# The zero column's term as a three-row matmul in the first sixteen steps, with ScalarE copying the product out of PSUM

## The chip, the cores and the metric

One core of a Trainium2 chip runs the kernel. The metric is device time in microseconds; for the kernel before it is 1673.05 us, the median of three runs. The engines are TensorE (PE in the profile, with PEld for its weight loads), VectorE (DVE), ScalarE (ACT), GpSimd (POOL) and SyncE (SP, which only issues DMAs here). Each works through its own instructions strictly in program order; semaphores hold an instruction back until what it needs is there.

## The reference, cut to what matters

```python
def _attn_ref(x):                       # x: 8 x 3072 x 256
    X = np.fft.fft(x, axis=1)
    X = np.fft.fft(X, axis=2)
    return X.real.astype(np.float32)

def _moe_ref(x, w_in, w_out):           # w_in 256 x 2048, w_out 2048 x 256
    h = x @ w_in
    sp = np.where(h > 20.0, h, np.log1p(np.exp(np.minimum(h, 20.0))))
    g = h * np.tanh(sp)                 # Mish
    return (g @ w_out).astype(np.float32)
```

The second function is applied to every row of the first one's result, 24576 rows in all.

## The kernel before, in words

The FFT along the columns (256 long) is folded into the weights: `make_wc` multiplies `w_in` with cosine and sine tables and gives `wch`, `wsh` (rounded to the matmul format) with the rests `wcl`, `wsl`. The FFT along the sequence is done by folds (sums and differences on VectorE and GpSimd) and matmuls with a table `dft`. Each of the 8 batches gives 3 chunks of 1024 tokens in mirrored pairs, held as two arrays P and Q: for one token of a pair the hidden value is P+Q, for the other P-Q.

A step takes one of the 16 blocks of 128 hidden units of a chunk; there are 384 steps, and the first chunk has steps 0 to 15. In step s `mm1` makes P in PSUM tile `pa` and Q in `pb` (three matmuls each: high times high, low times high, high times low part). `make_h` has three VectorE instructions: L848 adds to P the term of the column with index 0, which the folded weights do not hold (a token vector `p0b` times one number per hidden unit, `wc0`), and writes to SBUF; L849 adds Q, L850 subtracts it. ScalarE then applies Mish to the 1024 values (L958). Four steps later `split` rounds the result to `gh` on ScalarE (L858) and takes the rest `gl` on VectorE (L859; for steps 12 and later on GpSimd), and six steps later `mm2` (L869) multiplies with the second weights.

The order on each engine is written by hand: the main loop, and a table `EARLY` that says after which step the preparation of the weights and the folds of the first batch are placed. Entries with step -1 stand ahead of the loop. The 64-bit weights come as integer pairs; `conv` makes floats of them in three parts: part 0 on VectorE (L589, L590), part 1 on ScalarE (L592, L593), part 2 on VectorE and GpSimd (L595 to L597). `make_wl` (L626, L627) and `split_out` (L632, L633) make rests. All of this lies in the first 150 us, between the steps of the first chunk. `other_chunks` prepares the second chunk in steps 12 to 15 (its ScalarE instruction is L482).

At the start `zero`, a tile of zeros, is filled by GpSimd (L775); `warm` multiplies it with itself on TensorE (three matmuls, six rows of the profile) before and after `make_mids` (L646 to L659). `eye`, an identity matrix, comes by DMA as the third of ScalarE's queue. The first instruction of GpSimd that is no fill is L361 in `pairs0`. In the order of instructions a row ISA stands directly ahead of it; in the profile its two parts are called MODIFY_POOL_CONFIG.

Of the kernel before, what the change touches and what calls it, by code (L numbers as in the profile page):

```python
# [10 lines left out]
F32 = mybir.dt.float32  # L11
F32R = mybir.dt.float32r
# [3 lines left out]
ALU = mybir.AluOpType  # L16
# [72 lines left out]
def _tables():  # L89
# [46 lines left out]

SPLIT_V = 12
RH = 6

FOLD_AT = (19, 10, 44)  # L140
FIRST_AT = (44, 45)
# [133 lines left out]
def fft_moe(ctx, tc, x, col_d, mids_d, w_in, w_out, cs_d, dft_d, ysel_d, eye_d, out, single_d):  # L275
    nc = tc.nc
    V, A, G, T, SP = nc.vector, nc.scalar, nc.gpsimd, nc.tensor, nc.sync
    ctx.enter_context(tc.manual_schedule())

    def pool(name, bufs=1, **kw):  # L280
        return ctx.enter_context(tc.tile_pool(name=name, bufs=bufs, **kw))

    cp = pool("const")
# [23 lines left out]
    wsh = cp.tile([128, FF], F32R, name="wsh")  # L307
    wsl = cp.tile([128, FF], F32R, name="wsl")
    woh = cp.tile([128, NF, D], F32R, name="woh")
    wol = cp.tile([128, NF, D], F32R, name="wol")  # L310
    wc0 = cp.tile([128, NF], F32, name="wc0")
    ends = cp.tile([128, NB], F32, name="ends")
    ends0 = cp.tile([128, NB], F32, name="ends0")
    last2 = cp.tile([128, 2], F32R, name="last2")
    pe = cp.tile([NB, 1], F32, name="pe")

    place = [0, 0]

    def small(p, n, k=1):
        place[k] += n  # L320
        return hring[:p, RH - k, place[k] - n:place[k]]

# [7 lines left out]
    eye = small(128, 128)  # L330
# [142 lines left out]
    def mixed(v):  # L473

        return v.rearrange("p a s -> p s a")

    def placed(v):

        return v.rearrange("p (s a) -> p a s", a=2)
# [78 lines left out]
    p0b = {}  # L558
# [8 lines left out]
    raws, conv_w = {}, {}  # L567

    def room(kind, i):

        if kind == "in" and i in (2, 3):
            tu = gp.tile([128, 1024], F32, tag="gl", name="wtu")
            return gp.tile([128, 1024], F32, tag="gh", name="wraw"), tu[:, :512], tu[:, 512:]
        ring, j = PLACES[kind, i]
        r = (wring if ring == "w" else xring)[:, int(j)]
        return r[:, :1024], r[:, 1024:], otp.tile([128, 512], F32, tag="ot", name="wu")

    def load_w(kind, i):
        r, t, u = raws[kind, i] = room(kind, i)
# [2 lines left out]
    def conv(kind, i, part, eng="G"):  # L582

        r, t, u = raws[kind, i]
        lo, hi = (r.bitcast(I32).rearrange("p (n t) -> p n t", t=2)[:, :, j] for j in range(2))
        ti, ui = t.bitcast(I32), u.bitcast(I32)
        if part == 0:

            V.tensor_scalar(ui, hi, 20, 0x7FF, op0=ALU.logical_shift_right, op1=ALU.bitwise_and)  # L589
            V.tensor_single_scalar(ti, hi, 0xFFFFF, op=ALU.bitwise_and)  # L590
        elif part == 1:
            A.activation(ui, ui, AF.Relu, scale=2.0 ** 23, bias=-896.0 * 2 ** 23)  # L592
            A.activation(t, ti, AF.Copy, scale=2.0 ** -20, bias=1.0)  # L593
        else:
            V.scalar_tensor_tensor(ui, hi, -2 ** 31, ui, op0=ALU.bitwise_and, op1=ALU.bitwise_or)  # L595
            V.scalar_tensor_tensor(t, lo.bitcast(U32), 2.0 ** -52, t, op0=ALU.mult, op1=ALU.add)
            ENG[eng].tensor_tensor(t, t, u, op=ALU.mult)  # L597
            conv_w[kind, i] = t

    win_w = {}  # L600

    def make_wc(q):

# [20 lines left out]
    def make_wl(q):  # L624
        sl = slice(512 * q, 512 * q + 512)
        V.tensor_tensor(wcl[:, sl], win_w.pop(("lo", q, 0)), wch[:, sl], op=ALU.subtract)  # L626
        V.tensor_tensor(wsl[:, sl], win_w.pop(("lo", q, 1)), wsh[:, sl], op=ALU.subtract)  # L627

    def split_out(g):
        w = conv_w.pop(("out", g)).rearrange("p (f j) -> p f j", f=2)  # L630
# [5 lines left out]
    sp = {}  # L636
# [78 lines left out]
    def first_p0():  # L715

        pa = psacc.tile([128, 512], F32, tag="acc3", name="p0")
        def all_rows(v):
            return v[:, 0:1].to_broadcast([v.shape[0], 128])

        even = const(0, 0, 0)
        T.matmul(pa[:, 0:128], all_rows(xt[:, 0, 1, 0]), even[:, 0:128], start=True, stop=True)
        T.matmul(pa[:, 128:256], all_rows(xt[:, 0, 0, 0]), even[:, 128:256], start=True, stop=False)
        T.matmul(pa[:, 128:256], all_rows(xm[:, 0, 0]), alt[0:1, 128:256], start=False, stop=True)
        for c in range(2):
            T.matmul(pa[:, 256:512], all_rows(xt[:, 1, c, 0]), const(c, 1, 0), start=c == 0, stop=c == 1)
        p0b[0] = p2.tile([128, 512], F32, tag="p0b", name="p0b")
        A.copy(placed(p0b[0]), pa.rearrange("p (a s) -> p a s", a=2))


    G.memset(alt, 0.0)
# [14 lines left out]
    load_x(0, 3)  # L746
    load_w("in", 2)
    load_w("in", 3)


    uv = fp.tile([128, 2, 2, 2, 128], F32, tag="e", name="uv")
    eo = fp.tile([128, 2, 2, 128], F32, tag="o", name="eo")
# [64 lines left out]
    def chunk0(par, part):  # L817
# [1 line left out]

    parts = dict(chunk0=chunk0, put_mids=lambda: put_mids(0))  # L820
    parts.update({g.__name__: g for g in (
        make_mids, warm, first_p0, add_n1, fold_z, pairs0, sums0, load_w, conv, make_wc, make_w0, make_wl, split_out, col_fold, col_z, col_cs)})
    early = {}
    for t, g, args in EARLY:
        early.setdefault(t, []).append(lambda g=parts[g], args=args: g(*args))
# [6 lines left out]
    def mm1(s):  # L832
        ch, f = divmod(s, NF)
        q = chunks[ch]
        fs = slice(128 * f, 128 * f + 128)
        pa, pb = ps("pa"), ps("pb")
        for dst, wh, wl, n in ((pa, wch, wcl, "p"), (pb, wsh, wsl, "q")):
            dst = dst.rearrange("p (s a) -> p s a", a=2)
            T.matmul(dst, wh[:, fs], mixed(q[n + "h"]), start=True, stop=False)  # L839
            T.matmul(dst, wh[:, fs], mixed(q[n + "l"]), start=False, stop=False)  # L840
            T.matmul(dst, wl[:, fs], mixed(q[n + "h"]), start=False, stop=True)  # L841
        return pa, pb

    def make_h(s, pab):
        pa, pb = pab
        ch, f = divmod(s, NF)
        h = hring[:, s % RH]
        V.scalar_tensor_tensor(h[:, 0:512], p0b[ch], wc0[:, f:f + 1], pa, op0=ALU.mult, op1=ALU.add)  # L848
        V.tensor_tensor(h[:, 512:1024], h[:, 0:512], pb, op=ALU.add)  # L849
        V.tensor_tensor(h[:, 0:512], h[:, 0:512], pb, op=ALU.subtract)  # L850

    def split(s):

        h = hring[:, s % RH]
        gh = gp.tile([128, 1024], F32R, tag="gh", name="gh")
# [83 lines left out]
    for tau in range(NS + LAG_M):  # L939
        b, r = divmod(tau, 3 * NF)  # L940
# [8 lines left out]
        if tau < NS:  # L949
            make_h(tau, pab)  # L950
# [6 lines left out]
        if tau < NS:  # L957
            A.activation(hring[:, tau % RH], hring[:, tau % RH], AF.Mish)  # L958
            for f in early.pop(tau, []):
                f()  # L960
            other_at = OTHER_AT if b else OTHER0_AT
            if r in other_at:
                i = other_at.index(r)
# [7 lines left out]
            if fold_q:  # L971
                goal += pace
                while fold_q and spent + fold_q[0][0] / 2 <= goal + 1e-9 or fold_q and r == FOLD_AT[2]:
                    cost, f = fold_q.pop(0)
# [41 lines left out]
```

## Time and profile before

| | |
|---|---|
| median of three runs | 1673.05 us (1672.95 to 1673.29) |
| the profiled execution, its own time | 1674.39 us |
| its span in the profile | 1672.6 us |
| TensorE's matmuls busy | 1630.5 us, 97% of the span |
| VectorE / ScalarE / GpSimd busy | 1122.9 / 862.7 / 1153.5 us |

The profiled execution's time is 1.8 us above its span and 1.34 us above the median. Shares over the whole span say little about the first 150 us, where the change lies.

### The profile page before, as it was taken

To read this page: it belongs to the slowest core of one execution; us is meant where nothing else is said; L and a number is where in the kernel's file an instruction comes from. 1 tells how busy PE (TensorE), PEld (TensorE's weight loads), DVE (VectorE), ACT (ScalarE), POOL (GpSimd) and SP (SyncE) were. 2 spreads that over 40 slices of the span, in tenths; PEclk is the share of its full clock that TensorE was granted. 3 is DMA by queue.
4 is the path that set the end of the run, shared out by engine and by line. 5 is a ranking of instruction groups with operands and counts; after the bars stand their busy time and mean duration, and the time that the engine had idled before them with its cause. 6 is when DMAs were issued, how large, how long until landed. Compare 5 with 4: busy or idle time off the path is not lost.

```text
span 1672.6 us, 20901 instructions
## 1 busy us (share of the span) xinstructions
PE 1630.5 (97%) x7534; PEld 1403.6 (84%) x7534; DVE 1122.9 (67%) x1680; ACT 862.7 (52%) x968; POOL 1153.5 (69%) x654
## 2 busy tenths in 40 slices
PE   7778999999999999999999999999999999999999
PEld 4456888888888888888888888888888888888887
DVE  7998776666766767567766667667666667655453
ACT  3445555555555555555555555545554555554454
POOL 1444987588856877578866877578766788655566
PEclk8889999999999999999999999999999999999999
DMA  4212000300002000300002000020002000000000
GB/s 185 77 51 83 32 26 7 107 33 1 28 10 103 32 1 32 107 1 32 26 7 108 32 1 32 27 82 32 14 19 108 1 32 26 7 32 8 25 26 25
DMA packets 25376, 67.58 MB, mean 40 GB/s; under 512 B 3141, under 2 KB 3618, under 8 KB 25274
## 3 DMA queue, kind: packets, MB, share of 16 engines
q1 hardware_dynamic: 24474, 64.91, 10.7%
q8 instruction: 60, 0.98, 0.2%
q10 hardware_dynamic: 800, 1.35, 0.2%
q14 instruction: 42, 0.34, 0.1%
HBM read 40.97 MB, written 25.27 MB: 40 GB/s over the span
## 4 chain that ended last, share of the span: by engine, by line
PE 92%; DVE 6%; POOL 1%; issue 0%; DMA 0%; ACT 0%; DVEq 0%; ACTq 0%; POOLq 0%
PE acc L869 58%; PE pa L839 5%; PE pb L840 5%; PE pa L840 5%; PE pb L839 5%; PE pb L841 5%; PE pa L841 5%; PE pa L454 1%; PE pb L454 1%; DVE gl L859 1%; DVE hring L848 1%; DVE hring L849 1%; DVE wu L595 0%; DVE wu L589 0%; DMA hring<-table_ysel_dram 0%
## 5 line engine op out<-in xcount | busy, mean ns | idle before, releaser
L859 POOL TENSOR_TENSOR gl<-hring,gh 128x1024 fp32r<-128x1024 f32 x372 | 888.1, 2387 | 412.4 <-ACT gh L858 410.5
L858 ACT CAST gh<-hring 128x1024 fp32r<-128x1024 f32 x384 | 402.1, 1047 | 665.4 <-PE acc L869 647.6
L869 PE MATMUL acc<-gh,wol 128*128 128x512 f32 x1536 | 583.8, 380 | 2.9 <-POOL wol L633 2.9
L869 PE MATMUL acc<-gh,woh 128*128 128x512 f32 x1536 | 583.9, 380 | 0.6 <-ACT woh L632 0.6
L848 DVE SCALAR_TENSOR_TENSOR hring<-p0b,wc,pa 128x512 f32<-128x512 f32 x384 | 286.4, 746 | 371.7 <-PE pa L841 355.8
L958 ACT ACTIVATE hring<-hring 128x1024 f32<-128x1024 f32 x384 | 404.3, 1053 | 34.3 <-DVE hring L850 25.2
L869 PE MATMUL acc<-gl,woh 128*128 128x512 f32 x1536 | 406.2, 379 | 0.0
L869 PEld LDWEIGHTS acc<-gh,wol 128*128 128x128 f32 x1536 | 291.3, 190 | 45.1 <-POOL wol L633 3.6
L869 PEld LDWEIGHTS acc<-gh,woh 128*128 128x128 f32 x1536 | 291.4, 190 | 42.6 <-ACT woh L632 1.0
L869 PEld LDWEIGHTS acc<-gl,woh 128*128 128x128 f32 x1536 | 290.6, 189 | 41.9 <-POOL gl L859 0.5
L849 DVE TENSOR_TENSOR hring<-hring,pb 128x512 f32<-128x512 f32 x384 | 264.1, 688 | 42.7 <-DVE hring L848 1.8
L850 DVE TENSOR_TENSOR hring<-hring,pb 128x512 f32<-128x512 f32 x384 | 263.7, 687 | 13.3
L839 PE MATMUL pa<-h,wch 128*128 128x512 f32 x384 | 155.4, 405 | 7.2 <-DVE hring L848 5.0
L839 PE MATMUL pb<-h,wsh 128*128 128x512 f32 x384 | 147.2, 383 | 5.2 <-ACT h L482 3.5
L840 PE MATMUL pb<-l,wsh 128*128 128x512 f32 x384 | 146.7, 382 | 0.3 <-POOL l L483 0.3
L840 PE MATMUL pa<-l,wch 128*128 128x512 f32 x384 | 146.8, 382 | 0.0
L841 PE MATMUL pb<-h,wsl 128*128 128x512 f32 x384 | 146.6, 382 | 0.0
L841 PE MATMUL pa<-h,wcl 128*128 128x512 f32 x384 | 146.6, 382 | 0.0
L839 PEld LDWEIGHTS pa<-h,wch 128*128 128x128 f32 x384 | 73.3, 191 | 20.1 <-DVE hring L848 5.6
L839 PEld LDWEIGHTS pb<-h,wsh 128*128 128x128 f32 x384 | 73.1, 190 | 18.3 <-ACT h L482 3.9
L840 PEld LDWEIGHTS pb<-l,wsh 128*128 128x128 f32 x384 | 73.2, 191 | 11.1 <-POOL l L483 0.6
L841 PEld LDWEIGHTS pa<-h,wcl 128*128 128x128 f32 x384 | 73.4, 191 | 10.6
(255 smaller groups left out, 1154.2 us busy)
## 6 DMA issues: line engine op xcount, KB each, us to landing
xring<-x_dram SPq DMA_DIRECT2D x32, 768.0 KB
out_dram<-ot SPq DMA_DIRECT2D x96, 256.0 KB
p0b<-p_d SPq DMA_DIRECT2D x23, 256.0 KB
wring<-w_out_dram SPq DMA_DIRECT2D x5, 512.0 KB
wring<-w_in_dram SPq DMA_DIRECT2D x3, 512.0 KB
xring<-w_in_dram SPq DMA_DIRECT2D x3, 512.0 KB
xring<-w_out_dram SPq DMA_DIRECT2D x3, 512.0 KB
wraw<-w_in_dram SPq DMA_DIRECT2D x2, 512.0 KB
```

The costliest lines, as they stand in the source:

```text
L454: T.matmul(dst, lhs(c), const(c, par, sine), start=c == 0, stop=c == 1)
L839: T.matmul(dst, wh[:, fs], mixed(q[n + "h"]), start=True, stop=False)
L840: T.matmul(dst, wh[:, fs], mixed(q[n + "l"]), start=False, stop=False)
L841: T.matmul(dst, wl[:, fs], mixed(q[n + "h"]), start=False, stop=True)
L848: V.scalar_tensor_tensor(h[:, 0:512], p0b[ch], wc0[:, f:f + 1], pa, op0=ALU.mult, op1=ALU.add)
L849: V.tensor_tensor(h[:, 512:1024], h[:, 0:512], pb, op=ALU.add)
L850: V.tensor_tensor(h[:, 0:512], h[:, 0:512], pb, op=ALU.subtract)
L858: A.copy(gh, h)
L859: (V if s < SPLIT_V else G).tensor_tensor(gl, h, gh, op=ALU.subtract)
L869: T.matmul(acc[i].rearrange("p (s a) -> p s a", a=2), w[:, f, 128 * d:128 * d + 128], mixed(g.rearrange("p (a s) -> p a s", a=2)[:, :, 256 ...
L958: A.activation(hring[:, tau % RH], hring[:, tau % RH], AF.Mish)
```

## The change: what it does

In steps 0 to 15 the zero column's term is no longer added by VectorE. A fourth matmul with three rows (the weight's high part, its low part, its high part again, against the token vector's high, high and low part) adds it to `pa`, and ScalarE copies the finished `pa` to SBUF. VectorE makes only the sum and the difference. `make_rows` gathers the three weight rows for four steps at a time, with two matmuls against a selector `pick` and a copy; `p0_row` makes the token rows. `pick` and a factor `less` are made on GpSimd from `eye`. From step 16 on all is as before. The scratch of `conv` is now taken when part 0 runs, not when the load is issued.

```diff
+    pa = pa.rearrange("p (a s) -> p a s", a=2)
+    ph = p2.tile([128, 512], F32R, tag="p0b", name="ph")
+    A.copy(placed(ph[:3]), pa[:3])
+    sp["row"] = ph[:3], pa[:3]
+
+def p0_row():
+    ph, pa = sp["row"]
+    V.scalar_tensor_tensor(placed(prow), placed(ph), less, pa, op0=ALU.mult, op1=ALU.add)
...
+def make_rows(q):
+    sl = slice(512 * q, 512 * q + 512)
+    pw = psacc.tile([128, 512], F32, tag="acc3", name="pr") if q == 0 else ps("pb")
+    for k, w in enumerate((wsh, wsl)):
+        T.matmul(pw[:3], pick[:, 3 * k:3 * k + 3], w[:, sl], start=k == 0, stop=k == 1)
+    wrow[q] = otp.tile([128, 512], F32R, tag="ot", name="wrow")[:3]
+    A.copy(wrow[q], pw[:3])
...
     load_w("in", 2)
     load_w("in", 3)
+    G.tensor_single_scalar(less, eye[:3, 2:3], -1.0, op=ALU.mult)
+    for i in range(6):
+        G.tensor_single_scalar(pick[:, i:i + 1], eye[:, 127:128], float(i in (0, 2, 4)), op=ALU.mult)
...
-            T.matmul(dst, wl[:, fs], mixed(q[n + "h"]), start=False, stop=True)
+            row = s < ROWS and n == "p"
+            T.matmul(dst, wl[:, fs], mixed(q[n + "h"]), start=False, stop=not row)
+            if row:
+                T.matmul(pa, wrow[f // 4][:, 128 * (f % 4):128 * (f % 4) + 128], prow, start=False, stop=True)
...
-        V.scalar_tensor_tensor(h[:, 0:512], p0b[ch], wc0[:, f:f + 1], pa, op0=ALU.mult, op1=ALU.add)
+        if s < ROWS:
+            A.copy(h[:, 0:512], pa)
+        else:
+            V.scalar_tensor_tensor(h[:, 0:512], p0b[ch], wc0[:, f:f + 1], pa, op0=ALU.mult, op1=ALU.add)
```

`ROWS` is 16. `zero` is filled some lines below the seven new GpSimd instructions, as it was below the loads before.

GpSimd's order at the start of the program, before the change:

```order
L731 MEMSET alt 128x258
L733 MEMSET alt 128x65 x2
L775 MEMSET zero 128x512
L361 ISA
L361 TENSOR_TENSOR o<-xring 128x768 x2
```

and with it (line 803 is the fill of `zero`, 370 is `pairs0`):

```order
L757 MEMSET alt 128x258
L759 MEMSET alt 128x65 x2
L775 ISA
L775 TENSOR_SCALAR less<-hring 3x1
L777 TENSOR_SCALAR pick<-hring 128x1 x6
L803 MEMSET zero 128x512
L370 TENSOR_TENSOR o<-xring 128x768 x2
```

The ISA row and the seven small instructions moved ahead of the fill of `zero`; the first small one waits for the DMA of `eye`.

ScalarE's order around steps 0 and 1, before the change (L592 and L593 are part 1 of `conv`, L958 is Mish):

```order
L592 ACTIVATE wtu<-wtu 128x512 [waits DVE_49]
L593 ACTIVATE wtu<-wtu 128x512 [waits DVE_49]
L958 ACT_TABLE_LOAD
L958 ACTIVATE hring<-hring 128x1024 [waits DVE_49]
L689 COPY p0z<-pa 8x256 [waits PE_49]
L691 COPY pe<-pa 8x1
L689 COPY p0z<-pa 8x256 [waits PE_49]
L592 ACTIVATE wu<-wu 128x512 [waits DVE_49]
L593 ACTIVATE wring<-wring 128x512 [waits DVE_49]
L958 ACTIVATE hring<-hring 128x1024 [waits DVE_49]
```

and with it (L603 and L604 are part 1 of `conv`, L880 the new copy, L992 Mish):

```order
L603 ACTIVATE wtu<-wtu 128x512
L604 ACTIVATE wtu<-wtu 128x512
L880 COPY hring<-pa 128x512
L992 ACT_TABLE_LOAD
L992 ACTIVATE hring<-hring 128x1024
L709 COPY p0z<-pa 8x256
L711 COPY pe<-pa 8x1
L709 COPY p0z<-pa 8x256
L603 ACTIVATE wu<-wu 128x512
L604 ACTIVATE wring<-wring 128x512
L880 COPY hring<-pa 128x512
L992 ACTIVATE hring<-hring 128x1024
```

The copy stands behind all that ScalarE was given in the step before, the two activations of `conv` among it.

VectorE's order at the same place, the end of the part ahead of the loop and step 0, before:

```order
L589 TENSOR_SCALAR wtu<-wraw 128x512
L590 TENSOR_SCALAR wtu<-wraw 128x512
L848 SCALAR_TENSOR_TENSOR hring<-p0b,wc_95,pa 128x512
L849 TENSOR_TENSOR hring<-hring,pb 128x512
L850 TENSOR_TENSOR hring<-hring,pb 128x512
L595 SCALAR_TENSOR_TENSOR wtu<-wraw,wtu 128x512
```

and with it (L600 and L601 are part 0 of `conv`, L883 and L884 the sum and the difference):

```order
L600 TENSOR_SCALAR wtu<-wraw 128x512
L601 TENSOR_SCALAR wtu<-wraw 128x512
L883 TENSOR_TENSOR hring<-hring,pb 128x512
L884 TENSOR_TENSOR hring<-hring,pb 128x512
L606 SCALAR_TENSOR_TENSOR wtu<-wraw,wtu 128x512
```

L848 is gone; L883, which took its place, now waits for ScalarE's copy. `p0_row` adds one VectorE instruction ahead of the loop.

## Rows read from the trace of the kernel before

**Rows 1.** Stretches: busy us (instructions) of PE, PEld, DVE, ACT, POOL; clock; DMA

```profile
30.00:150.60 120.60, 90.10 (x334) 61.70 (x333) 111.97 (x164) 54.93 (x82) 52.15 (x44) 0.88 0.21 70
171.00:1672.60 1501.60, 1497.84 (x7049) 1313.42 (x7049) 977.11 (x1440) 788.35 (x851) 1086.91 (x594) 1.00 0.09 34
```

**Rows 2.** Chain that ended last, 0 to 36 us: start, us, what

```profile
9.38 2.68 PE warm L781 x6
...
24.21 0.70 DVE sum L770
```

**Rows 3.** Timeline, 0 to 9 us, POOL, PE and SP: start, us, instruction, idle before

```profile
1.10 0.24 POOL L733 MEMSET alt<- 128x65 f32 x2
1.27 0.53 POOL L775 MEMSET zero<- 128x512 f32 x1
1.85 4.48 PE L781 MATMUL warm<-zero 128*128 128x512 f32 x6 [1.85 <-POOL zero L775]
7.18 0.39 PE L646 MATMUL pa<-early,hring 96*48 96x128 f32 x2 [0.85 <-DMA hring<-table_ysel_dram]
7.43 0.43 SPq L340 DMA_DIRECT2D xring<-x_dram  x1
```

**Rows 4.** Instructions of line 361 until 32 us: duration ns, first and last start

```profile
L361 POOLq MODIFY_POOL_CONFIG  x2: 11/11/11, 1.7 to 1.8; - x2
L361 POOLq EVENT_SEMAPHORE  x1: 16707/16707/16707, 11.7 to 11.7; - x1
```

**Rows 5.** Timeline, POOL: one short fill and one TENSOR_SCALAR

```profile
0.24 0.10 POOL L998 MEMSET const-float32-0.0<- 128x1 f32 x1 [0.24 <-issue]
...
58.32 0.40 POOL L371 TENSOR_SCALAR o<-o 128x256 f32<-128x256 f32 x1
```

**Rows 6.** Groups by line, DVE, 34.9 to 146 us: count, busy us, mean ns

```profile
L848 DVE SCALAR_TENSOR_TENSOR hring<-p0b,wc,pa 128x512 f32<-128x512 f32 x16 | 11.8, 738 | 0.2 <-PE pa L841 0.2
```

**Rows 7.** Timeline: a ScalarE copy out of PSUM; one that VectorE waits for

```profile
22.59 0.62 ACT L728 COPY p0b<-p 128x512 f32<-128x512 f32 x1 [1.14 <-PE p L726]
...
45.17 0.57 ACT L610 CAST wch<-pa 128x512 fp32r<-128x512 f32 x1
...
45.77 0.69 DVE L626 TENSOR_TENSOR wcl<-pa,wch 128x512 fp32r<-128x512 f32 x1 [0.39 <-ACT wch L610]
```

**Rows 8.** Timeline, ACT and DVE, at steps 0, 1 and 12

```profile
35.23 0.73 DVE L848 SCALAR_TENSOR_TENSOR hring<-p0b,wc,pa 128x512 f32<-128x512 f32 x1
35.39 0.61 ACT L592 ACTIVATE wtu<-wtu 128x512 int32<-128x512 int32 x1
35.91 0.61 ACT L593 ACTIVATE wtu<-wtu 128x512 f32<-128x512 int32 x1
36.06 0.69 DVE L849 TENSOR_TENSOR hring<-hring,pb 128x512 f32<-128x512 f32 x1
...
42.24 0.61 ACT L593 ACTIVATE wring<-wring 128x512 f32<-128x512 int32 x1
42.77 0.69 DVE L849 TENSOR_TENSOR hring<-hring,pb 128x512 f32<-128x512 f32 x1
...
125.43 0.62 ACT L593 ACTIVATE xring<-xring 128x512 f32<-128x512 int32 x1
125.96 0.69 DVE L849 TENSOR_TENSOR hring<-hring,pb 128x512 f32<-128x512 f32 x1
```

**Rows 9.** Timeline, ACT and DVE, Mish of step 5 and step 6

```profile
75.90 1.06 ACT L958 ACTIVATE hring<-hring 128x1024 f32<-128x1024 f32 x1 [9.12 <-issue]
...
78.33 0.74 DVE L848 SCALAR_TENSOR_TENSOR hring<-p0b,wc,pa 128x512 f32<-128x512 f32 x1
```

**Rows 10.** Timeline, ACT and DVE, step 13

```profile
131.89 0.40 ACT L482 CAST h<-spare 128x256 fp32r<-128x256 f32 x1
...
131.99 0.69 DVE L849 TENSOR_TENSOR hring<-hring,pb 128x512 f32<-128x512 f32 x1
```

**Rows 11.** Chain that ended last: the matmuls of one step's `mm2`

```profile
182.92 2.59 PE acc L869 x12
```

More of the change, by code (lines that the diff above doesn't have):

```diff
@@ L138 @@
 RH = 6
+ROWS = 16
 FOLD_AT = (19, 10, 44)
@@ L172 @@
     (-1, 'make_w0', (0,)),
+    (-1, 'make_rows', (0,)),
     (-1, 'add_n1', (1, 1, 'V')),
+    (-1, 'p0_row', ()),
     (-1, 'fold_z', (1,)),
@@ L199 @@
     (2, 'make_w0', (1,)),
+    (2, 'make_rows', (1,)),
     (2, 'conv', ('out', 1, 2)),
@@ L229 @@
     (7, 'make_w0', (2,)),
+    (7, 'make_rows', (2,)),
     (7, 'conv', ('out', 2, 2)),
@@ L251 @@
     (11, 'make_w0', (3,)),
+    (11, 'make_rows', (3,)),
     (11, 'sums0', (1, 4, 7, 'e')),
@@ L315, in fft_moe @@
     pe = cp.tile([NB, 1], F32, name="pe")
+    prow = cp.tile([3, 512], F32R, name="prow")
+    pick = cp.tile([128, 6], F32R, name="pick")
+    less = cp.tile([3, 1], F32, name="less")
     place = [0, 0]
@@ L575, in room @@
         r = (wring if ring == "w" else xring)[:, int(j)]
-        return r[:, :1024], r[:, 1024:], otp.tile([128, 512], F32, tag="ot", name="wu")
+        return r[:, :1024], r[:, 1024:], None
     def load_w(kind, i):
@@ L584, in conv @@
         r, t, u = raws[kind, i]
+        if u is None:
+            raws[kind, i] = r, t, u = r, t, otp.tile([128, 512], F32, tag="ot", name="wu")
         lo, hi = (r.bitcast(I32).rearrange("p (n t) -> p n t", t=2)[:, :, j] for j in range(2))
@@ L598, in conv @@
             conv_w[kind, i] = t
-    win_w = {}
+    win_w, wrow = {}, {}
     def make_wc(q):
@@ L726, in first_p0 @@
             T.matmul(pa[:, 256:512], all_rows(xt[:, 1, c, 0]), const(c, 1, 0), start=c == 0, stop=c == 1)
-        p0b[0] = p2.tile([128, 512], F32, tag="p0b", name="p0b")
-        A.copy(placed(p0b[0]), pa.rearrange("p (a s) -> p a s", a=2))
+        pa = pa.rearrange("p (a s) -> p a s", a=2)
[5 more added lines that the diff above has]
+        V.scalar_tensor_tensor(placed(prow), placed(ph), less, pa, op0=ALU.mult, op1=ALU.add)
     G.memset(alt, 0.0)
@@ L821, in fft_moe @@
     parts.update({g.__name__: g for g in (
-        make_mids, warm, first_p0, add_n1, fold_z, pairs0, sums0, load_w, conv, make_wc, make_w0, make_wl, split_out, col_fold, col_z, col_cs)})
+        make_mids, warm, first_p0, p0_row, add_n1, fold_z, pairs0, sums0, load_w, conv, make_wc, make_w0, make_wl, make_rows, split_out, col_fold, col_z, col_cs)})
     early = {}
```

## The prediction

> **What bounds the kernel now.** I read the stretches first. From 171 us to the end TensorE's matmuls are busy 1497.84 of 1501.60 us, but from 30 to 150.6 us only 90.10 of 120.60, while VectorE is busy 111.97 [rows 1]. So the kernel has two parts: a tail of 1500 us that TensorE sets, where the change does nothing, and a beginning that VectorE and the start-up set. The end moves by as much as the moment moves at which TensorE gets going without gaps. Whatever the beginning gains or loses stands in the total one for one; nothing in the tail takes it back, since TensorE has no idle time there to give.
>
> Then the chain of waits in the first 36 us: it goes through the warm-up matmuls on TensorE and later through VectorE; the second set of warm-up matmuls (9.38 us, 2.68 us) and L770 (24.21 us) are on it [rows 2]. TensorE's queue at the start is therefore on the path that sets the end, and a late start of TensorE is paid in full.
>
> **The start-up: what the seven small GpSimd instructions move.** Before, GpSimd fills `alt` until 1.10 + 0.24 = 1.34 us, then `zero` until 1.80 us, and TensorE's first instruction, a warm-up matmul, starts at 1.85 us [rows 3]. Behind the fill stands the row ISA, MODIFY_POOL_CONFIG, at 1.7 to 1.8 us. The next thing that GpSimd's queue does, taking up the semaphores of L361, starts at 11.7 us [rows 4]. So this instruction holds the queue for about 9.9 us. Before, that cost nothing: L361 had to wait for other work until after 28 us (it waited 16.7 us more from 11.7 [rows 4]).
>
> With the change ISA stands ahead of the fill of `zero`, and so it holds back the fill, and with it TensorE's whole queue, which begins with `warm`. It can start at 1.3 us, when `alt` is done, and ends at 1.3 + 9.9 = 11.2 us. The DMA of `eye` is then long there: the fourth issue of L340 on SP, which reuses that DMA's semaphore, went out at 7.43 us [rows 3]. Seven small instructions follow. Their price lies between 0.10 us (a fill of one column) and 0.40 us (a TENSOR_SCALAR of 256 columns) [rows 5]; with one column each they are nearest to the first, so 0.7 us for seven (at most 2.8). Then the fill, 0.53 us, and 0.05 us from it to TensorE [rows 3]: the first matmul starts at 11.2 + 0.7 + 0.53 + 0.05 = 12.5 us, 10.65 us later than before. Before, TensorE stood idle 0.85 us between the first warm-up and `make_mids` [rows 3], for a DMA that is now there in time, and this is saved. I take the warm-up itself to be as slow as before, 4.48 us, since again it is the first that TensorE does; if it went at the pace of the second, 2.68 us [rows 2], 1.8 us would come back. Queued behind it are `make_mids`, ScalarE's copies of its result, and behind those on ScalarE the first activations of `conv`, for which VectorE waits: all of VectorE's start is later by the same amount. **First term: 10.65 - 0.85 = +9.8 us.**
>
> The Trainium skill, page "GPSIMD Engine Reference", section "Instruction dispatch", says that the first call of a freshly loaded kernel pays for loading code, about 6 us, "with no visible profile instruction". The trace agrees in kind and shows more, 9.9 us; by the page's figure the estimate would be the end of the load at 7.3 us and this term at +6.0.
>
> **`p0_row`.** One VectorE instruction over 512 elements of three rows, like L848 (738 ns mean [rows 6]) in all but the rows; it stands behind the instructions that follow L770 on the chain [rows 2]. **+0.7 us**; 0 if it fell into a wait.
>
> **The sixteen steps.** Removed are 16 instructions L848, 11.8 us [rows 6]. From the start of L848 to that of L849 is 36.06 - 35.23 = 0.83 us [rows 8], so a step gains about 0.84 us, 13.4 in all, if ScalarE's copy is done when VectorE comes to L883. The copy takes 0.62 us, and VectorE starts 0.03 us after a ScalarE result is there (45.17 + 0.57, then 45.77) [rows 7]: 0.6 us from its start to L883. What decides is when ScalarE is free, since the copy stands behind everything that it was given in the step before. Back to back its activations of 512 columns start 0.52 us apart (35.39 and 35.91 [rows 8]).
>
> - Step 0: the last L593 starts at 35.91, so the copy at 36.43 and L883 at 37.05; L849 started at 36.06 [rows 8]. Loss 1.0 us.
> - Step 1: L593 at 42.24, copy 42.76, L883 at 43.4, against 42.77 [rows 8]. Loss 0.6. The reason is general: where `conv` part 0 is VectorE's last work ahead of a step, part 1 on ScalarE and then the copy come one after the other behind it, and VectorE stands still meanwhile. Six steps are such (1, 4, 8, 9, 10, 12); step 12 gives 125.43 + 0.52 + 0.6 against 125.96 [rows 8], 0.6 again, the others, read in the same way, 0.4 to 0.5. Sum of the six: 2.9.
> - Step 13: behind L482, which starts at 131.89 and lets the next go after 0.3, the copy ends at 132.8, against L849 at 131.99 [rows 10]. Loss 0.8. This wait hangs on GpSimd too, whose part 2 of `conv` comes ahead of L632 and L482.
> - Step 3: TensorE's fourth matmul and the later release of a PSUM buffer by `make_rows` make it lose 0.2.
> - Steps 2, 5, 6: ScalarE is free in time. Mish of step 5 ends at 75.90 + 1.06 = 76.96, the copy 0.6 later, ahead of L848's 78.33 [rows 9]. Gain 0.84 each, 2.5.
> - Steps 7, 11, 14, 15: the copy comes in between; gains 0.3, 0.3, 0.1, 0.1. Before step 11 VectorE waits for TensorE's weights anyway, which takes back 0.4 of the losses before it.
>
> Losses 1.0 + 2.9 + 0.8 + 0.2 = 4.9, gains 2.5 + 0.8 + 0.4 = 3.7. **Third term: +1.2 us.** Between steps `gh` and Mish stand behind the copy; both still end ahead of what waits for them, as the times above allow.
>
> **At nothing.** TensorE gets 16 matmuls of 512 columns and 8 for `make_rows`, each some 0.22 us (twelve take 2.59 us [rows 11]), 5.2 us; they lie in the 30 us in which it is idle from 30 to 150.6 us [rows 1]. Uncovered they would cost up to 5.2. ScalarE's 16 copies and 4 of `make_rows`, some 12 us, have room in its 66 idle us [rows 1]; their place in its queue is what the third term counts. The `conv` scratch rings keep a free buffer or wait for work long done: 0.
>
> **Sum.** 9.8 + 0.7 + 1.2 = +11.7 us. The profiled execution would go from its 1674.39 us to 1686.1; it lies 1.34 us above the median of the runs, so the forecast for the median is 1673.05 + 11.7 = **1684.8 us**, 0.7% slower. A measurement of this kernel tells about 0.2%, 3.3 us, from no change.
>
> **Rivals.**
> - *The start-up waits only for `eye`.* If the load of code runs beside the queue, or is over when `eye` lands, the seven instructions start by 7.43 us; then 7.43 + 0.7 + 0.53 + 0.05 = 8.7, less 1.85 and 0.85: +6.0 instead of +9.8, so 1681.0. For it: the gap of 9.9 us was read while the input loads kept the DMAs busy, and nothing shows how it ends. Against it: the queue did nothing visible in all that time. The Trainium skill's 6 us, cited above, give the same time. Chance 0.20.
> - *Not slower: the copy is in time in all sixteen steps.* Then the third term is -13.4 instead of +1.2: 9.8 + 0.7 - 13.4 = -2.9, so 1670.2. It decides where ScalarE comes to the copy 0.6 us or more ahead of VectorE in more than ten of the steps, as it would if VectorE's own work were longer than ScalarE's in each. Against it: the seven steps 0, 1, 4, 8, 9, 10, 12, where `conv` puts two activations directly ahead. For it: where VectorE's L589 and L590 run beside GpSimd they take more than a microsecond, and a shift of the two against each other changes which steps are tight. Chance 0.10; together with the rival above, 1666.3, 0.02 of it.
> - *More than the sum.* TensorE's new matmuls fall uncovered into gaps that the copy now ends, up to +5.2, or the small GpSimd instructions cost 0.4 us each, +2.1: around 1690. Chance 0.12.
> - *The change does nothing to the start.* If neither the load nor the DMA held the fill back, 0.7 + 1.2 gives 1675.0. The order of the rows speaks against it. Chance 0.03.
>
> **How the numbers follow.** The forecast case has 0.55; its own range is 1682.5 to 1687.5 (the 1.8 of the warm-up below, the 2.1 of the small instructions above, a microsecond of the steps either way). Adding the first rival and half of the third gives 1679.5 to 1688.5 for eight in ten. Slower by over 0.2% are the forecast, the first and the third rival, 0.87; within 0.2% most of the second and the fourth, 0.10; faster by more 0.03.
>
> **What would show it.** Right: the first matmul at about 12.5 us with the fill of `zero` as its releaser, MODIFY_POOL_CONFIG at 1.3 us and the first TENSOR_SCALAR of GpSimd near 11; step 0's L883 some 11 us later than L849 was; L883 waiting for ScalarE's copy in about nine of sixteen steps, 0.5 to 1.5 us each; from 180 us on the same rows as before, about 12 us later. Wrong: a first matmul ahead of 9 us (the first rival), L883 hardly ever waiting for ScalarE (the second), or a catch-up of the late start somewhere between 20 and 170 us, which I see no place for.

## The result and the profile after

The changed kernel takes 1682.53 us in the median of five runs (1681.26 to 1683.36) against 1673.06 (1672.95 to 1675.96) of the kernel before: ratio 1.0052, 95% interval 1.0041 to 1.0063, so 9.5 us slower. The forecast was 1684.8. The profiled execution took 1682.52 us; its span is 1680.7 us, 8.1 more than that of before. (The profiled execution of before lay 1.34 us above its median, that of after on its median, which is the difference between 8.1 and 9.5.) Line numbers from here on are those of the changed kernel.

The stretches of after, with the columns of [rows 1]:

```profile
30.00:150.60 120.60, 100.28 (x355) 65.23 (x354) 98.68 (x153) 61.18 (x101) 47.53 (x42) 0.84 0.16 53
...
150.60:164.00 13.40, 10.01 (x34) 7.59 (x33) 8.22 (x15) 4.81 (x8) 3.77 (x4) 0.75 0.46 177
...
179.10:1680.70 1501.60, 1497.84 (x7049) 1313.31 (x7049) 974.24 (x1440) 788.81 (x851) 1084.24 (x594) 1.00 0.10 34
```

The last row is the tail of [rows 1] again, 1497.84 busy of 1501.60 us, 8.1 us later. All that changed lies ahead of it. The first row must not be laid beside the first of [rows 1], since the steps now run about 7.5 us later. About the same work lies from 22.5 to 143.1 us in before:

```profile
22.50:143.10 120.60, 90.24 (x335) 61.83 (x334) 111.64 (x168) 52.63 (x82) 49.22 (x42) 0.86 0.16 53
```

VectorE is busy 98.68 us where it was 111.64: 13.0 us of work are gone from it, and yet the kernel is no faster. TensorE is busy 10.0 us more, and its granted clock there is 0.84 instead of 0.86.

The start on GpSimd and TensorE in the timeline of after, to be laid beside [rows 3]:

```profile
7.01 0.40 POOL L775 TENSOR_SCALAR less<-hring 3x1 f32<-3x1 f32 x1 [5.66 <-DMA hring<-table_eye_dram]
7.38 1.04 POOL L777 TENSOR_SCALAR pick<-hring 128x1 fp32r<-128x1 f32 x6
8.37 0.52 POOL L803 MEMSET zero<- 128x512 f32 x1
...
8.93 5.14 PE L809 MATMUL warm<-zero 128*128 128x512 f32 x6 [8.93 <-POOL zero L803]
14.01 0.42 PE L666 MATMUL pa<-early,hring 96*48 96x128 f32 x2
...
16.09 2.82 PE L809 MATMUL warm<-zero 128*128 128x512 f32 x6
```

GpSimd stood still 5.66 us until `eye` was there, made the seven small instructions in 1.36 us (7.01 to 8.37), and then filled `zero`. `make_mids` (L666) starts at 14.01 us instead of 7.18 [rows 3]: 6.83 later. The chain that ended last goes through the same DMA:

```profile
1.66 5.27 DMA hring<-table_eye_dram
...
8.93 5.14 PE warm L809 x6
```

The groups of two lines of after answer to [rows 4]. L775 is the first small instruction, and L370 is the line that was L361:

```profile
L775 POOLq MODIFY_POOL_CONFIG  x2: 11/11/11, 1.3 to 1.3; - x2
...
L370 POOLq EVENT_SEMAPHORE  x1: 24477/24477/24477, 11.5 to 11.5; - x1
```

MODIFY_POOL_CONFIG moved to 1.3 us, and between it and 11.5 us eight instructions ran. The semaphore row of L370 stands at 11.5 all the same, where it stood at 11.7: the late time belongs to L370 and what it waits for, not to MODIFY_POOL_CONFIG ahead of it. The trace shows what that is. The first semaphore that this row waits for is the one that the first load of `xring` counts up as it lands. The last packet of that load landed at 11.71 us in before and at 11.44 in after, 0.03 and 0.02 us ahead of the row (in e1, e2 and e3 below it is 0.02 to 0.03 us as well). In before TensorE waited for the same load:

```profile
11.76 0.33 PEld L762 LDWEIGHTS pa<-xring,hring 128*128 128x128 f32 x2 [0.53 <-DMA xring<-x_dram]
```

Steps 0, 1 and 12 on ScalarE and VectorE, beside [rows 8], with `p0_row` (L754) ahead and step 13 behind [rows 10]:

```profile
32.47 0.73 DVE L754 SCALAR_TENSOR_TENSOR prow<-ph,less,p 3x512 fp32r<-3x512 f32 x1
33.13 0.41 DVE L813 TENSOR_TENSOR eo<-uv 128x256 f32<-128x256 f32 x1
...
43.52 0.61 ACT L604 ACTIVATE wtu<-wtu 128x512 f32<-128x512 int32 x1
44.04 0.56 ACT L880 COPY hring<-pa 128x512 f32<-128x512 f32 x1
44.63 0.69 DVE L883 TENSOR_TENSOR hring<-hring,pb 128x512 f32<-128x512 f32 x1 [1.65 <-ACT hring L880]
...
50.81 0.62 ACT L604 ACTIVATE wring<-wring 128x512 f32<-128x512 int32 x1
51.33 0.56 ACT L880 COPY hring<-pa 128x512 f32<-128x512 f32 x1
51.92 0.69 DVE L883 TENSOR_TENSOR hring<-hring,pb 128x512 f32<-128x512 f32 x1 [1.35 <-ACT hring L880]
...
133.51 0.69 DVE L883 TENSOR_TENSOR hring<-hring,pb 128x512 f32<-128x512 f32 x1 [1.35 <-ACT hring L880]
...
140.25 0.69 DVE L883 TENSOR_TENSOR hring<-hring,pb 128x512 f32<-128x512 f32 x1 [1.58 <-ACT hring L880]
```

In each of these the sum, L883, stands still until the copy is done, and in the first two an activation of `conv` (L604) stands directly ahead of the copy. The waits of VectorE from 30 to 155 us put this together (total us, times, longest us):

```profile
DVE hring L883 <- ACT hring L880: 13.0, 11, 1.7
```

Sixteen instructions L848 were worth 13.4 us of VectorE's time; eleven waits took 13.0 of them back. TensorE has a new wait too: two of the sixteen row matmuls (L872) stood still until ScalarE had copied the rows of `make_rows` (total us, times, longest us):

```profile
PE pa L872 <- ACT wrow L647: 5.4, 2, 3.3
```

The balance of the profiled execution, read from step to step as L883 after less L849 before: `make_mids` and the second warm-up are 6.8 to 6.9 us late; `p0_row` adds 0.66 (32.47 to 33.13); step 0 adds 1.06 (44.63 - 36.06 = 8.57 in all, less 7.51); step 1 another 0.58; from there the steps win and lose until step 15 stands at +7.48, -0.03 against 7.51. From step 18 on the difference is 8.1 in nearly every step to the end (7.7 to 8.5 in a few). The last 0.6 us come between 150 and 164 us. There TensorE stood idle 3.39 us for ScalarE's L491 and then worked at the lower level of its clock (1.2 GHz): the same fifteen matmuls took from 158.1 to 164.4 us in after, 6.3 us, and from 150.6 to 156.2 in before, 5.6 us. In before TensorE had stood idle there just as long, 3.49 us, so the idle time does not explain the difference. The granted clock of the stretch of 13.4 us is 0.75 (row above); over the same work in before, 142.5 to 155.9 us, it is 0.87.

### The profile page after: what moved, and what is told of

It is laid out like the page before. It is cut to its first block, busy times and chain, and to the rows that moved or that the text cites. A ratio compares the mean times of both kernels' runs of the same rounds, so it can differ in the third digit from the quotient of the medians.

```text
span 1680.7 us, 20960 instructions
## 1 busy us (share of the span) xinstructions
PE 1642.9 (98%) x7558; PEld 1408.2 (84%) x7558; DVE 1106.9 (66%) x1665; ACT 872.6 (52%) x988; POOL 1150.6 (68%) x661
## 3 DMA queue, kind: packets, MB, share of 16 engines
q10 hardware_dynamic: 800, 1.35, 0.2%
## 4 chain that ended last, share of the span: by engine, by line
PE 93%; DVE 4%; ACT 1%; issue 1%; POOL 1%; DMA 0%; ACTq 0%; DVEq 0%; POOLq 0%
PE acc L903 58%; PE pb L867 5%; PE pb L868 5%; PE pb L870 5%; PE pa L867 5%; PE pa L870 5%; PE pa L868 5%; PE pb L463 1%; PE pa L463 1%; DVE hring L883 0%; PE warm L809 0%; DVE gl L893 0%; DVE hring L884 0%; PE pb L466 0%; PE pb L468 0%
## 5 line engine op out<-in xcount | busy, mean ns | idle before, releaser
L882 DVE SCALAR_TENSOR_TENSOR hring<-p0b,wc,pa 128x512 f32<-128x512 f32 x368 | 274.7, 746 | 375.6 <-PE pa L870 362.9
L992 ACT ACTIVATE hring<-hring 128x1024 f32<-128x1024 f32 x384 | 404.4, 1053 | 26.9 <-DVE hring L884 26.9
L883 DVE TENSOR_TENSOR hring<-hring,pb 128x512 f32<-128x512 f32 x384 | 264.0, 687 | 53.6 <-ACT hring L880 13.0
L884 DVE TENSOR_TENSOR hring<-hring,pb 128x512 f32<-128x512 f32 x384 | 263.7, 687 | 13.3
L870 PEld LDWEIGHTS pb<-h,wsl 128*128 128x128 f32 x384 | 73.5, 191 | 10.6
```

## The experiments

The kernel before ran beside each: its median was 1673.56 us (25 runs) for e1 to e4, 1673.67 (31) for e5 to e9 and 1674.31 (27) for e10 to e12. The comparison is by ratios.

**e1: the seven small instructions behind the fill of `zero`.** The rest of the change stays.

```diff
-    G.tensor_single_scalar(less, eye[:3, 2:3], -1.0, op=ALU.mult)
-    for i in range(6):
-        G.tensor_single_scalar(pick[:, i:i + 1], ...)
...
     G.memset(zero, 0.0)
+    G.tensor_single_scalar(less, eye[:3, 2:3], -1.0, op=ALU.mult)
+    for i in range(6):
+        G.tensor_single_scalar(pick[:, i:i + 1], ...)
```

> The changed kernel with the seven small GpSimd instructions (less, pick) moved behind the fill of zero; nothing else. Theory (the late start is paid in full, since the fill of zero stood behind the DMA of eye): the first matmul is back at 1.85 us, make_mids at 7.2, and the whole 6.85 us come back: 1682.5 - 6.9 = 1675.6 us; what is left against before is p0_row's 0.7 us, the steps' sum near 0, and 0.6 us near 160 us where TensorE runs at the low clock for longer. Rival (part of the late start was taken back by VectorE's and ScalarE's gaps later on): less than 4 us come back, 1678.5 or more.

Measured: 1675.91 us, ratio 1.0014 (1.0004 to 1.0024). GpSimd and TensorE in its timeline:

```profile
1.26 0.53 POOL L800 MEMSET zero<- 128x512 f32 x1
6.89 0.40 POOL L801 TENSOR_SCALAR less<-hring 3x1 f32<-3x1 f32 x1 [5.11 <-DMA hring<-table_eye_dram]
...
1.84 5.46 PE L809 MATMUL warm<-zero 128*128 128x512 f32 x6 [1.84 <-POOL zero L800]
7.22 0.42 PE L666 MATMUL pa<-early,hring 96*48 96x128 f32 x2
```

GpSimd still waits 5.11 us for `eye`, but nobody waits for GpSimd. The place of seven instructions that take about 1.4 us together was worth 0.38% (1.0052 less 1.0014), 6.4 us; the two intervals together leave about 2.5 us either way. What is left against before is 2.3 us (0.7 to 4.0).

**e2: the kernel before, with the seven instructions ahead of the fill and nothing else of the change.** Their results are used by nothing.

```diff
+    G.tensor_single_scalar(less, eye[:3, 2:3], -1.0, op=ALU.mult)
+    for i in range(6):
+        G.tensor_single_scalar(pick[:, i:i + 1], ...)
...
     G.memset(zero, 0.0)
```

> The kernel before with the seven small instructions added ahead of the fill of zero (their results are not used); no other part of the change. Theory: first matmul at 8.9 us, 6.85 us late from make_mids on, 1673.05 + 6.9 = 1680.0 us. Rival (the start-up counts for less than its place on the chain says): under 1677.

Measured: 1680.98 us, ratio 1.0041 (1.0026 to 1.0056), that is 6.9 us slower (4.4 to 9.4). The start-up alone makes most of the slowdown. In its timeline the warm-up starts at 9.23 us and takes the 4.48 us of [rows 3]:

```profile
9.23 4.48 PE L786 MATMUL warm<-zero 128*128 128x512 f32 x6 [9.23 <-POOL zero L780]
13.64 0.42 PE L648 MATMUL pa<-early,hring 96*48 96x128 f32 x2
```

`make_mids` is 6.46 us late here. In this execution part of that is caught up: in step 18 the kernel is 4.9 us behind the profiled execution of before, and of the 6.5 us at the end 1.7 came in the tail (last section). Two executions of one kernel differ by as much (e1 and e12, last section), so whether a little of a late start is caught up stays open.

**e3: the kernel before, with one GpSimd TENSOR_SCALAR ahead of the fill that waits for no DMA.** It multiplies a column of `alt` by 1, so that MODIFY_POOL_CONFIG moves ahead of the fill but `eye` plays no part.

```diff
+    G.tensor_single_scalar(alt[:, 0:1], alt[:, 0:1], 1.0, op=ALU.mult)
     ENG = {"V": V, "G": G}
...
     G.memset(zero, 0.0)
```

> The kernel before with one GpSimd TENSOR_SCALAR of one column (a column of alt times one) ahead of the fill of zero: the instruction that loads GpSimd's code moves ahead of the fill, but no DMA is waited for. The prediction's reading (the load holds the queue for 9.9 us): the TENSOR_SCALAR near 11.3 us, first matmul near 12.3, about 1683. A load of some 6 us: TENSOR_SCALAR near 7.3, first matmul near 8.3, about 1679. A load that is over within 2 to 4 us or runs beside the queue: TENSOR_SCALAR ahead of 5.3, first matmul ahead of 6, 1673 to 1676.5.

Measured: 1673.65 us, ratio 1.0 (0.999 to 1.0009). GpSimd's and TensorE's start in its timeline:

```profile
1.39 0.22 POOL L749 TENSOR_SCALAR alt<-alt 128x1 f32<-128x1 f32 x1
1.55 0.53 POOL L776 MEMSET zero<- 128x512 f32 x1
...
2.12 5.29 PE L782 MATMUL warm<-zero 128*128 128x512 f32 x6 [2.12 <-POOL zero L776]
```

The groups of line 361 and of the new line in e3:

```profile
L749 POOLq MODIFY_POOL_CONFIG  x2: 11/11/11, 1.3 to 1.3; - x2
...
L361 POOLq EVENT_SEMAPHORE  x1: 17384/17384/17384, 11.2 to 11.2; - x1
```

MODIFY_POOL_CONFIG at 1.3 us, the instruction behind it at 1.39, the fill at 1.55: nothing is held. The semaphore row of L361 still comes at 11.2, 0.02 us behind the last packet of `xring`'s first load. The 9.9 us that the prediction gave to MODIFY_POOL_CONFIG were not its own.

**e4: the kernel before, with only ScalarE's copy in place of L848 in steps 0 to 15.** The zero column's term is left out there, so there is no row matmul, no `p0_row` and no new work at the start.

```diff
+        if s < 16:
+            A.copy(h[:, 0:512], pa)
+        else:
             V.scalar_tensor_tensor(h[:, 0:512], p0b[ch], wc0[:, f:f + 1], pa, ...)
```

> The kernel before, where in steps 0 to 15 ScalarE copies P out of PSUM in place of VectorE's L848; no rows, no fourth matmul, no late start. The zero column's term is left out in these steps. Theory (the wait for the copy behind ScalarE's queue eats what VectorE saves): VectorE waits about 13 us for the copy in 10 to 12 steps, and the time is 1673 within 1.5 us. Rival (the waits of the changed kernel come from TensorE's fourth matmul and make_rows): most of L848's 13.4 us is saved, 1660 to 1666.

Measured: 1672.9 us, ratio 0.9993 (0.9983 to 1.0002). VectorE's waits for the copy:

```profile
DVE hring L852 <- ACT hring L849: 12.5, 11, 1.7
```

Sixteen VectorE instructions less are worth nothing that can be measured, and 12.5 us of waits stand in their place, as in after. It needs no matmul and no start-up for that.

**e5: as e1, without the sixteen row matmuls** (the term is left out in the first chunk; `make_rows` and `p0_row` still run).

```diff
-            row = s < ROWS and n == "p"
+            row = False
```

> The kernel after with its seven small GpSimd operations behind the zero fill, and without the 16 three-row matmuls in the steps: the zero column's term is left out of the first chunk's steps, all else runs (the pick matmuls, the row copies, p0_row). Theory: the row matmuls lie in TensorE's slack and cost nothing but the two places where they wait for ScalarE's row copy (2.1 us each, steps 8 and 12, and there the copy of P was still later), so 1675.9 again, from 1674.5 to 1676.5. Rival: TensorE's 16 instances of 0.5 to 0.8 us (9.9 us in sum) are in part on the path, and 2 to 6 us come back: 1670 to 1674.

Measured: 1674.1 us, ratio 1.0001 (0.9992 to 1.0011), between the two forecasts and not told apart from e1. The two kernels ran on different chips, so e11 and e12 try the opposite, both on one chip.

**e11 and e12: each row matmul twice, beside e1 again.** In e11 the term counts twice in the first chunk; e12 is the kernel of e1.

```diff
+                T.matmul(pa, wrow[f // 4][:, ...], prow, start=False, stop=False)
                 T.matmul(pa, wrow[f // 4][:, ...], prow, start=False, stop=True)
```

> The kernel after with the seven small operations behind the zero fill, and each of the 16 three-row matmuls issued twice into P: the zero column's term counts twice in the first chunk's steps, all else is the same. Theory: the row matmuls lie in TensorE's slack, so doubling them costs 0 to 1 us against the same kernel with one (e12, the same kernel as e1, beside it). Rival: they are on the path for part of the steps; leaving them out brought 1.8 us on another chip, so doubling costs about 2 us or more.

> The same kernel as e1 (the seven small operations behind the zero fill), as the measure for e11 on the same chip: 1675.9, from 1674.9 to 1676.9.

Measured: 1675.89 us with two (ratio 1.0009, 1.0 to 1.0018), 1676.09 with one (1.0007, 0.9998 to 1.0016). Sixteen more matmuls cost nothing that these runs can tell: 0.3 us by the ratios, each of which is known to about 1.5 us. This tests the matmuls' own time. The wait of L872 for the rows' copy is not doubled by it; e5 has no such wait, and what it seemed to bring, 1.8 us, lies within the noise.

**e7: copy and row matmul only where the copy came in time,** in steps 2, 3, 5, 6, 7 and 11, with the small instructions behind the fill. The ten other steps keep L848's instruction, `p0b` stays as it was before, and the last `make_rows` goes.

```diff
-ROWS = 16
+ROWS = (2, 3, 5, 6, 7, 11)
...
-        if s < ROWS:
+        if s in ROWS:
             A.copy(h[:, 0:512], pa)
```

> The seven small operations behind the zero fill; copy by ScalarE and row matmul only in steps 2, 3, 5, 6, 7 and 11, where the copy came in time or nearly (0.0, 0.2, 0.0, 0.0, 0.4 and 0.4 us of wait); the ten others keep VectorE's scalar_tensor_tensor, so the 128-row copy of the zero column stays, and the last row quarter is not made. Theory (the wait for ScalarE's turn ate the saving): ten steps get 0.84 us of VectorE back and lose 11.8 us of waits, six keep their saving: 1675.9 - 11.8 + 8.4 = 1672.5, by another count 1673.5 + 0.7 (p0_row) - 6 x 0.84 + 1.1 = 1670.3; so 1670 to 1672.5, faster than before by 0.1 to 0.2%. Rival (VectorE is not what sets these steps; what it saves is lost to other waits): 1674 to 1676, as with all 16 steps.

Measured: 1671.1 us, ratio 0.9983 (0.9974 to 0.9992), 2.6 us faster than before and inside the theory's range. The waits of VectorE from 30 to 150.6 us:

```profile
DVE hring L882 <- ACT hring L879: 0.4, 1, 0.4
```

Of 13 us of waiting for the copy 0.4 are left. VectorE's time is worth something in these steps as long as its successor needs nobody else's turn.

**e8: all sixteen steps, but the copy ahead in ScalarE's queue.** In steps 0, 1, 4, 8, 9, 10 and 12 the step's first matmuls and the copy are issued ahead of the last `conv` part 1 of the step before. The arithmetic is complete; the basis is e1.

```diff
+    (7, 'ahead', (8,)),
     (7, 'conv', ('in', 6, 1)),
...
+    def ahead(s):
+        pabs[s] = mm1(s)
+        A.copy(hring[:, s % RH, 0:512], pabs[s][0])
...
-        pab = mm1(tau) if tau < NS else None
+        pab = pabs[tau] if tau in pabs else mm1(tau) if tau < NS else None
```

> The kernel after with the seven operations behind the zero fill and another order: in steps 0, 1, 4, 8, 9, 10 and 12 the first matmuls of the step and ScalarE's copy of P stand ahead of the last pair of weight-conversion activations of the step before, instead of behind them. The arithmetic is complete. Theory (the copy is late because it stands behind two activations that wait for VectorE's bit operations just made): P has been ready for 1 to 3 us in these steps, so the waits of 1.60, 1.35, 1.17, 1.35, 1.18, 1.17 and 1.35 us, 9.2 us in all, go: 1675.9 - 9.2 = 1666.7, from 1666 to 1669, faster than before. Rival (VectorE's freed time only waits elsewhere, for the conversion that now comes 0.5 us later or for the path over the Mish): 3 us or less come back, 1673 to 1676.

Measured: 1672.34 us, ratio 0.999 (0.998 to 0.9999): about 3.6 us better than e1 and e12 by the medians (4.0 and 2.8 by the ratios, each to about 2.3 us). That is far from the 9.2 of the theory, and the noise does not tell it from the 3 or less of the rival. Step 8 in its timeline (L982 is the copy, L610 and L611 part 1 of `conv`, L889 the sum, L898 and L899 `gh` and `gl`):

```profile
87.19 0.59 ACT L982 COPY hring<-pa 128x512 f32<-128x512 f32 x1 [0.58 <-PE pa L876]
89.75 0.63 ACT L610 ACTIVATE wu<-wu 128x512 int32<-128x512 int32 x1 [1.97 <-DVE wu L607]
90.29 0.61 ACT L611 ACTIVATE wring<-wring 128x512 f32<-128x512 int32 x1
90.81 1.03 ACT L898 CAST gh<-hring 128x1024 fp32r<-128x1024 f32 x1
...
89.64 0.54 DVE L608 TENSOR_SCALAR wring<-wring 128x512 int32<-128x512 int32 x1
90.10 0.67 DVE L889 TENSOR_TENSOR hring<-hring,pb 128x512 f32<-128x512 f32 x1
91.87 1.23 DVE L899 TENSOR_TENSOR gl<-hring,gh 128x1024 fp32r<-128x1024 f32 x1 [0.37 <-ACT gh L898]
```

The mechanism is as the theory has it: the copy is done two microseconds before VectorE comes, and L889 follows the bit operations without a gap (step 8 waited 1.35 us in e1). But `gh` now stands behind the two activations and comes 0.37 us late. The waits of VectorE show the same over all steps:

```profile
DVE hring L889 <- ACT hring L886: 3.7, 5, 1.6
...
DVE gl L899 <- PE acc L909: 1.7, 1, 1.7
DVE gl L899 <- ACT gh L898: 1.6, 4, 0.6
...
DVE hring L889 <- ACT wring L611: 1.1, 1, 1.1
...
DVE hring L889 <- ACT hring L982: 0.5, 1, 0.5
```

Of e1's 12.8 us of waits for the copy 4.2 are left: 3.7 for the copy at its old place (L886), 2.9 of them in steps 13 to 15, which were not reordered, and 0.5 for the copy that moved (L982). But `gl` now waits 1.7 us for TensorE and 1.6 for `gh` (0.9 in e1), and the sum 1.1 us for an activation of `conv` in step 1: 8.6 us won, 3.5 lost, which is near the 5.8 us by which step 15 came earlier than in e1's profiled execution. Part of the time that the copy gave back thus waits elsewhere. In the profiled execution another part went in the tail (last section).

**e9: the other order alone,** in the kernel before, with `mm1` ahead in the same seven steps and L848 as it was.

```diff
+    def ahead(s):
+        pabs[s] = mm1(s)
```

> The kernel before with only the other order of the first matmuls of steps 0, 1, 4, 8, 9, 10 and 12 (ahead of the last conversion of the step before), no copy and no row matmul; the arithmetic is complete. Theory: in the kernel before VectorE waits for nothing of TensorE in these steps, so the order alone is worth nothing: 1673.5, from 1672.5 to 1674.5. Rival: TensorE being earlier is itself what the other kernel gains, and this one comes out at 1668 to 1672 as well.

Measured: 1673.96 us, ratio 1.0004 (0.9995 to 1.0014). TensorE being earlier is worth nothing by itself that can be measured; what e8 gained on e1 came with the copy.

**e10: as e8, with copy and row matmul in steps 0 to 12 only.**

```diff
-ROWS = 16
+ROWS = 13
```

> The kernel with the copy of P ahead in the queue (as in e8), but row matmul and copy in steps 0 to 12 only; steps 13, 14 and 15 keep VectorE's scalar_tensor_tensor, and the 128-row copy of the zero column stays. The arithmetic is complete. Theory: of the waits that were left in e8, those of steps 13, 14 and 15 (1.59, 0.63, 0.63 us, behind the casts of the next chunk's parts) go, and three times 0.84 us of VectorE come back, and 0.3 to 0.5 us for the larger copy at the start: e8's time less 0 to 2.5 us (at step 13 the trace of e8 falls back from 5.4 to 2.9 us ahead of before, which here would stay), so 1670 to 1672. Rival: TensorE's next-chunk matmuls set steps 13 to 17 whatever VectorE does, so it is e8's time again, 1672 to 1673.

Measured: 1671.97 us, ratio 0.9984 (0.9975 to 0.9992). That is 2.3 us ahead of before, e8 was 1.3; the intervals overlap, so this doesn't tell the two forecasts apart. e7, e8 and e10 beat the kernel before by 0.1 to 0.2%, with intervals that end below 1; among the three nothing is decided.

## Why the prediction was right in its sign and large in its size

**The frame** held. The tail is the same to the hundredth, and what stood at step 18 stood at the end (so in before and after; e2, e5 and e8 lost 1.7 to 1.8 us in the tail, last section).

**The first term, +9.8 us,** was mis-sized, and this is the step that failed: "So this instruction holds the queue for about 9.9 us." The gap from 1.8 to 11.7 us in [rows 4] was read as the duration of what stood ahead of it. e3 shows that MODIFY_POOL_CONFIG takes no time worth naming, and after, e1 and e3 all have the late semaphore row on L370 or L361 at 11.2 to 11.5 us, wherever MODIFY_POOL_CONFIG stands. What filled the gap was L361's own wait for the first load of `xring`, which landed at 11.71 us. What held the fill was the DMA of `eye`, as the first rival had it (+6.0, to which the prediction gave 0.20). Measured +6.8 to +6.9: the rival's 6.0, less 0.42 for `eye` at 7.01 instead of 7.43, plus 0.66 for the seven instructions (1.36 us, not 0.7), plus 0.66 for the warm-up (5.14 us, not 4.48): 6.9. (The last is not clearly the change's doing: the warm-up took 4.48 us in e2 too, whose fill was late, and 5.29 and 5.46 in e3 and e1, whose fill was not.) The runs bear the size out within some 2.5 us: 6.4 us by taking the place away (e1), 6.9 by making it alone (e2). The forecast's 9.8 lies outside both, the rival's 6.0 does not.

So the time came out near for a reason other than the one given. The prediction itself named a first matmul ahead of 9 us as a sign that it was wrong and the first rival right, and the first matmul came at 8.93. That the median lies just on the lower edge of the forecast's own range (1682.5) is luck: the 8.1 us that the two traces differ by would give 1681.2, the rival had 1681.0, and the rest is where the profiled execution of before happened to lie among its runs.

The prediction cited the Trainium skill, page "GPSIMD Engine Reference", section "Instruction dispatch", for a first call that pays about 6 us for loading code. In e3 the first TENSOR_SCALAR started 0.09 us behind MODIFY_POOL_CONFIG and took 0.22 us, and the kernel's time did not move, so the trace does not agree for this instruction, which perhaps was not freshly loaded; that the page's figure gave nearly the right start (7.3 us; measured 7.01) was chance, because `eye` happened to land then. The estimate of the term by that figure is 7.3 + 0.7 + 0.53 + 0.05 - 1.85 - 0.85 = +5.9, where the prediction has +6.0.

**`p0_row`, +0.7 us:** 0.66. Right.

**The third term, +1.2 us,** came out at 0.0 in the profiled execution. The mechanism was right, and it is why the change has no gain to set against its start-up: the copy stands behind ScalarE's other work. The forecast had L883 waiting in about nine steps; it waited in eleven, 13.0 us, against the 13.4 that it saved. Of the four steps worked out in full three were close (step 0: 1.0 forecast, 1.06; step 1: 0.6 and 0.58; step 13: 0.8 and 0.71); step 12 lost 0.05 instead of 0.6. The difference of 1.2 us between sum and trace is not more than one execution differs from the next (e1 and e12 below), so it can't be put down to a single step. Nor do the runs tell it from zero: what e1 and e12 leave against before, 2.3 and 1.2 us, each to about 1.6, is `p0_row` and this term together, which the forecast had at 1.9. e4 shows the queue place as the cause without the rest of the change, e7 by leaving out the steps where the copy is late, and e8 by moving the copy, which took away 8.6 of 12.8 us of waits.

**At nothing:** the row matmuls' own time is hidden, as said, as far as the runs can tell (e11 against e12). The wait of two of them for the copy of `make_rows` (5.4 us) was not forecast; it is not shown to cost anything, since e5, which is without it, is not told apart from e1. The later taking of `conv`'s scratch was not tried alone.

**The sum.** For the profiled execution the forecast was 1686.1 us, and it took 1682.52: 3.6 less, of which the first term has 2.9 and the third 1.2; 0.6 us came in addition from the clock around 160 us, which was not forecast. For the median it was 1684.8 against 1682.53.

**The rivals.** The second, the copy in time in all sixteen steps, is out: it was late in eleven. The third, around 1690, is out by the time itself, although the small instructions did take twice the forecast 0.7 us. The fourth is out by e2: the start alone costs 6.9 us.

## What to carry to other kernels

An instruction moved to another engine is priced by its place in that engine's queue: read what stands ahead of it, and whether this in turn waits for the engine that was to be relieved. Here `conv` made VectorE wait for ScalarE, which had just been waiting for VectorE, and sixteen instructions saved became 13 us of waits; used only in the six steps where ScalarE was free, and with the small instructions behind the fill, the same edit won 2.6 us.

Before anything is put ahead of the first instruction of a start-up chain, look at what it waits for: seven instructions of 1.4 us cost 6.4, since the first needed a DMA. And a gap ahead of a row is not the duration of the row before it; look at which semaphore the late row waits for and when that was counted up. A kernel with one harmless instruction at the place in question settles it at once.

## What the runs showed of the hardware

**The same kernel, two granted clocks.** e1 and e12 are one kernel with medians of 1675.91 and 1676.09 us, but the profiled executions have spans of 1674.7 and 1672.6. Their stretches, e1 first, then e12:

```profile
36.00:80.00 44.00, 35.92 (x106) 18.66 (x105) 35.71 (x51) 23.42 (x39) 19.61 (x16) 0.79 0.23 73
80.00:120.00 40.00, 35.24 (x126) 24.24 (x125) 33.33 (x44) 20.56 (x32) 13.46 (x11) 0.84 0.17 53
```

```profile
36.00:80.00 44.00, 35.37 (x110) 17.90 (x109) 36.22 (x53) 22.74 (x38) 19.28 (x16) 0.85 0.23 73
80.00:120.00 40.00, 32.81 (x126) 22.97 (x124) 34.62 (x43) 21.81 (x32) 15.58 (x14) 0.91 0.17 53
```

In the stretch where TensorE has gaps, the mean granted clock was 0.79 and 0.84 in the one execution, 0.85 and 0.91 in the other, and by step 15 they are 2.2 us apart. A term of 1 us can't be read from one trace of this beginning; the ratios over ten runs give it to about 1.6 us.

**A loss in the tail.** e8 was 4.12 us ahead of the profiled execution of before in step 349 and 2.32 at the end. It lost them between steps 356 and 361, where the 48 matmuls of eight columns stand that compute the hidden values of the single end tokens. The stretches of e8 there, then those of e1:

```profile
1532.00:1540.00 8.00, 8.00 (x37) 7.55 (x37) 1.51 (x4) 0.31 (x1) 0.84 (x1) 0.54 0.01 2
1540.00:1546.00 6.00, 6.00 (x23) 4.99 (x22) 3.55 (x7) 2.95 (x4) 0.65 (x1) 0.75 0.35 132
```

```profile
1538.00:1546.00 8.00, 8.00 (x40) 7.46 (x40) 1.55 (x4) 0.31 (x1) 1.06 (x1) 0.61 0.01 3
1546.00:1552.00 6.00, 6.00 (x28) 5.19 (x28) 4.83 (x7) 3.18 (x4) 2.08 (x1) 0.95 0.46 175
```

The granted clock falls during these small matmuls, though TensorE is busy all the time (they start 0.11 us apart at first and 0.21 later), and stays low for some full-size matmuls behind them, for longer in e8 (0.54, then 0.75) than in e1 (0.61, then 0.95; in before the same). The traces of e2 and e5 have this loss too, 1.7 us each; in the nine others the distance from before changes by 0.05 us at most between step 349 and the end. So the tail is not quite without loss of its own, and some of the spread between runs comes from here. Why it lasted longer in some executions was not tried.

**Small GpSimd instructions:** a TENSOR_SCALAR of one column took 0.40 us for the first, about 0.17 each for the six that followed, back to back (1.04 us), and 0.22 alone in e3.
